# A convolution mixer and a token MLP on one core: sine phases in 16 bit, other loads first, diagonals on GpSimd, and a new order of all engines

## The chip, the core and the metric

The kernel runs on one core of one Trainium2 chip. The core has five engines that run side by side, each through its own queue of instructions in order: TensorE (PE in the profile; PEld is its weight load), VectorE (DVE), ScalarE (ACT), GpSimd (POOL) and SyncE (SP), which here only issues transfers. POOL and ACT issue transfers too. Matrix products land in PSUM, eight banks of 512 float32 per partition, and must be copied out by DVE or ACT before the bank is free; everything else lies in one tensor in SBUF that the program calls `arena` (so nearly all tiles in the profile have this one name; PSUM is `ps`). The metric is the device time of one execution in microseconds (us), the median of several runs.

## The reference

Part A mixes along the sequence (2048 positions, 448 channels): a layer norm of q, a shift convolution with four taps of k, a product with v, a long convolution of that with a state kernel (done by real FFTs of length 4096), a skip term, and the gate by q. Part B is an MLP over the 2048 positions (2048 to 1792 to 2048) with a layer norm ahead and a gelu between.

```
def _A_ref(q, k, v, shift_k, ssm_k, ssm_D):
    k_shift = sum over t of k_pad[:, t:t + S, :] * shift_k[:, ks - 1 - t]
    kv = k_shift * v
    kv_f = rfft2(kv_pad)                  # length 2 * S along the sequence
    kf_f = rfft2(kf_pad)                  # of the state kernel
    y = irfft2(kv_f * kf_f)[:S]
    y = y + kv * ssm_D
    return q * y
...
h = x + _A_ref(_layernorm(x), A_k, A_v, A_shift_k, A_ssm_k, A_ssm_D)
h2 = h + _B_ref(_layernorm(h), B_w1, B_b1, B_w2, B_b2)
```

## The kernel before

The FFTs are matrix products in two stages of small transforms. The sequence lies as 128 partitions by 16 rows (`R` = 16), so a tile row is 128 positions by 448 channels. The stages, by the names that the step tables use:

- `tables` computes the transform tables on the chip. `E` (f16, 32 tiles of 128 columns) is the sine of a phase (an odd frequency times the position, modulo 8192; for the cosine 2048 more): DVE makes the phases as int32, ACT takes the sine (L837 to L847). `FW` is the table of the forward second stage, `MA`, `MB`, `MN` those of the inverse (L854 to L874, on POOL, DVE and ACT). `ID` is the identity for the transposes (L810), made from an iota (L789).
- `kT` transposes the state kernel by PE (L1037), `kv` transposes k (L965) into `KX`, convolves it with the four taps as products with diagonal matrices `DG` (L991; `DG` is made at L950 from the taps `wsc`, L943), and multiplies by v (L1006, DVE).
- `k1`, `u1`: first forward stage of the state kernel and of the signal (L1058; copied out by L1066 and L1068, then exchanged between partitions by 48 transfers each way, L1074, two of three on POOL and one on SP). Four buffers in SBUF take the copies, so the fifth group waits for transfers.
- `k2`, `u2`: second forward stage (L1093, needs `FW`; copied out by L738, L739, L741, L742).
- `i1`: the product of the two spectra (L1160, DVE, 16 of 1.08 us) and the first inverse stage (L1177), then an exchange by L1201 and, for the last rows, L1188.
- `i2`: second inverse stage (L1303, L1309), gate and residual, layer norm statistics and the normalised row `Q` (L1388). `q` are the statistics of the first layer norm (L1237 to L1260).
- `mlp`: first product (L1435 for 7 of 14 column blocks, row by row as `Q` comes; L1445 for the others), gelu (L1425), second product (L1457, 16 output rows of 14 products), the end of each row (L1460) and its store (L1468, L1471, L1465).

No planner decides at build time. Each instruction belongs to a step (`tables.6`, `kv.4`) and has a number in it; the table `ORDER` lists, for each engine, every instruction in the order of that engine's queue, and the table `SLOTS` says which PSUM bank each use takes. `_Sched` replays the tables, works out which semaphores each instruction must wait for, and emits the engines' programs. Which of DVE and ACT copies a PSUM bank out (`FX`) is set by the table in which the copy stands. An instruction that waits holds all that stands behind it on its engine.

Loads are issued by SP in the order of its table: two of the four pieces of k, the four of the state kernel, the row `ssm_D`, the two biases, the other k, v and the taps. `b2` is cast to float32 on DVE (L938). The first-layer weights (L1408, L1412) and the second-layer weights (L1419) follow late.

## Time and profile before

| what | us |
|---|---|
| median of 3 runs (170.71 to 171.06) | 170.73 |
| span of the profiled execution, first to last instruction | 168.7 |
| busy PE, DVE, ACT, POOL in that span | 160.0, 101.7, 90.3, 58.8 |
| PE starts the first product of the MLP | 78.26 |
| PE starts the second product | 123.70 |

The span lies inside the time of a run; what lies around it is 170.73 - 168.7 = 2.0 us. The profile has an entry for each instruction, named by its line, with its start, its duration and what ended the idle time of its engine before it. "Busy" of PE counts the pipeline's latency with each product, so PE may be called busy while it waits a little between short products. The granted TensorE clock is full (9 in each of 40 slices).

### The profile page before, as it was taken

Reading aid. Unit: us, or ns where it says so; the run is one execution under the profiler, and the core shown is the slowest. Engines: PE = TensorE matmul, PEld = TensorE weight load, DVE = VectorE, ACT = ScalarE, POOL = GpSimd, SP = SyncE. Lnnn points to the kernel's source line nnn. Section 1 sums busy time; section 2 is a strip of 40 time slices with the busy share of each in tenths; the row PEclk is TensorE's granted clock in tenths of the full one; section 3 lists DMA queues with packets and bytes.
Section 4 is the critical chain, followed back from the end, with each engine's and each line's share of the span. In section 5 each row is a group of like instructions: output and inputs, shape, how many; then the busy total and the mean of one; then the engine's idle time right before and its main releaser. Section 6 shows DMA issues by size and latency. Waiting matters only on the chain.

```text
span 168.7 us, 3563 instructions
## 1 busy us (share of the span) xinstructions
PE 160.0 (95%) x1416; PEld 92.4 (55%) x1416; DVE 101.7 (60%) x191; ACT 90.3 (54%) x130; POOL 58.8 (35%) x155
## 2 busy tenths in 40 slices
PE   6999999979989989889999999999999999999994
PEld 2776745434333333344554545555577777777783
DVE  7998999989999999999987440000002313132231
ACT  3699847989999999999675803103640000000000
POOL 8345727685830555675777330000000000000000
PEclk9999999999999999999999999999999999999999
DMA  4999899893659766658999999920000111101111
GB/s 142 421 310 385 286 278 348 312 355 132 211 134 325 248 197 186 196 152 290 388 402 400 424 421 422 418 112 0 0 0 12 46 54 54 54 2 56 54 54 54
DMA packets 15564, 35.15 MB, mean 208 GB/s; under 512 B 3804, under 2 KB 9644, under 8 KB 15548
## 3 DMA queue, kind: packets, MB, share of 16 engines
q1 hardware_dynamic: 12396, 28.26, 46.1%
q0 software_dynamic: 3008, 6.58, 12.1%
q8 instruction: 11, 0.18, 0.4%
q10 hardware_dynamic: 144, 0.08, 0.2%
q14 instruction: 5, 0.04, 0.1%
HBM read 22.05 MB, written 1.84 MB: 142 GB/s over the span
## 4 chain that ended last, share of the span: by engine, by line
PE 62%; ACT 15%; DVE 10%; DMA 6%; issue 3%; POOL 1%; DVEq 0%; ACTq 0%; POOLq 0%
PE ps L1457 25%; PE ps L1435 13%; PE ps L1445 13%; ACT arena L738 7%; DMA arena<-arena 6%; ACT arena L1068 4%; ACT arena L739 4%; DVE arena L1160 2%; PE ps L1309 2%; PE ps L1058 2%; PE ps L1037 2%; PE ps L1093 2%; DVE arena L741 2%; DVE arena L837 1%; PE ps L1177 1%
## 5 line engine op out<-in xcount | busy, mean ns | idle before, releaser
L1460 DVE SCALAR_TENSOR_TENSOR arena<-ps,arena 128x448 bf16<-128x448 f32 (+2 forms) x17 | 11.1, 656 | 55.8 <-PE ps L1457 55.8
L1457 PE MATMUL ps<-arena 128*128 128x448 bf16 (+2 forms) x238 | 42.7, 342 | 0.0
L1457 PEld LDWEIGHTS ps<-arena 128*128 128x128 bf16 x238 | 33.3, 145 | 9.5
L1435 PE MATMUL ps<-arena 128*128 128x448 bf16 x112 | 23.5, 353 | 0.0
L738 ACT CAST arena<-ps 128x896 bf16<-128x896 f32 (+1 forms) x29 | 23.1, 933 | 0.0
L1068 ACT CAST arena<-ps 128x896 bf16<-128x896 f32 x24 | 20.2, 920 | 4.8 <-PE ps L1058 3.3
L1445 PE MATMUL ps<-arena 128*128 128x448 bf16 x112 | 22.3, 352 | 0.0
L1074 POOL DMA_DIRECT2D arena<-arena x32 | 17.7, 558 | 8.6 <-ACT arena L1068 8.5
L1425 ACT ACTIVATE arena<-ps,arena 128x448 bf16<-128x448 f32 x14 | 8.2, 632 | 19.3 <-PE ps L1445 10.3
L1093 PE MATMUL ps<-arena 128*64 128x448 bf16 x128 | 15.3, 361 | 2.0 <-ACT arena L739 0.9
L1435 PEld LDWEIGHTS ps<-arena 128*128 128x128 bf16 x112 | 10.7, 98 | 10.8 <-DVE arena L1388 1.3
L1445 PEld LDWEIGHTS ps<-arena 128*128 128x128 bf16 x112 | 11.0, 98 | 10.2
L1160 DVE TENSOR_TENSOR arena<-arena 128x1792 bf16<-128x1792 bf16 x16 | 16.5, 1084 | 0.0
L1177 PE MATMUL ps<-arena 64*128 64x448 bf16 x128 | 14.1, 351 | 1.1 <-ACT arena L738 0.5
L1058 PE MATMUL ps<-arena 128*32 128x448 bf16 x256 | 14.6, 355 | 0.5 <-ACT arena L1068 0.2
L1201 POOL DMA_DIRECT2D arena<-arena x16 | 9.3, 586 | 13.8 <-ACT arena L738 12.9
L1093 PEld LDWEIGHTS ps<-arena 128*64 128x64 f16 x128 | 5.3, 108 | 11.2 <-ACT arena L739 3.4
L1177 PEld LDWEIGHTS ps<-arena 64*128 64x128 f16 x128 | 5.2, 94 | 9.8 <-DVE arena L1160 3.1
L1388 DVE TENSOR_SCALAR arena<-arena 128x448 bf16<-128x448 f32 x16 | 7.6, 509 | 4.8 <-POOL arena L1381 4.8
L1058 PEld LDWEIGHTS ps<-arena 128*32 128x32 f16 x256 | 5.1, 95 | 7.8 <-ACT arena L1068 2.6
L1237 DVE BATCH_NORM_STATS2 arena<-arena 128x6 f32<-128x448 bf16 x16 | 9.4, 612 | 0.0
L739 ACT ACTIVATE arena<-ps 128x896 bf16<-128x896 f32 x10 | 8.6, 926 | 0.8 <-PE ps L1093 0.8
(99 smaller groups left out, 189.4 us busy)
## 6 DMA issues: line engine op xcount, KB each, us to landing
arena<-in_B_w_dram SPq DMA_DIRECT2D x8, 896.0 KB, 10.2
arena<-in_B_w_dram SPq DMA_DIRECT2D x2, 2048.0 KB, 17.3
arena<-arena SPq DMA_DIRECT2D x16, 224.0 KB, 3.7
arena<-arena POOLq DMA_DIRECT2D x32, 112.0 KB, 3.9
arena<-in_B_w_dram SPq DMA_DIRECT2D x2, 1536.0 KB, 19.1
arena<-arena POOLq DMA_DIRECT2D x13, 196.0 KB, 3.7
arena<-in_A_k_dram SPq DMA_DIRECT2D x4, 448.0 KB, 5.9
arena<-in_A_v_dram SPq DMA_DIRECT2D x4, 448.0 KB, 9.1
```

The lines of the kernel that those rows point to most:

```text
L738: return e.copy(out=dst(), in_=src())
L739: return e.activation(out=dst(), in_=src(), func=ACT.Copy, scale=scale)
L1058: op("pe", lambda e, W, b=b, r=r, q=q, x=x, c0=c0: e.matmul(PS[32 * q:32 * q + 32, b.slots[x], 0:D], E[:, 2 * r + x, c0:c0 + 32], src[:, r ...
L1068: return e.copy(out=dst, in_=Ppair(b)) if W == "act" else e.tensor_copy(out=dst, in_=Ppair(b))
L1074: shuf[tag].append(op(q_, lambda e, W, g=g, i=i, a=a, nu=nu, jh=jh: e.dma_start(T[a + i:a + i + 4 * nu - 3:4].rearrange("p (j k) c d -> p ...
L1093: op("pe", lambda e, W, b=bs[h], h=h, j=j, c=c, par=par: e.matmul(PS[64 * par:64 * par + 64, b.slots[c], 0:D], FW[:, 64 * c:64 * c + 64], ...
L1160: op("dve", lambda e, W, m=m, i=i: e.tensor_tensor(out=MR(m.slots[0]).rearrange("p (x y) d -> p x y d", x=2), in0=TU[:, i].unsqueeze(2).br ...
L1177: k = op("pe", lambda e, W, b=bs[h], m=ms[h], par=par, t=t, tab=tab, xy=xy, P=P: e.matmul(Pb(b, par), tab[P, :], MR(m.slots[0])[P, xy, :], ...
L1435: op("pe", lambda e, W, r=r, fc=fc, b=bs[fc]: e.matmul(Pb(b), W1A[:, r, 128 * fc:128 * fc + 128], Q[:, r, :], start=(r == 0), stop=(r == R ...
L1445: op("pe", lambda e, W, r=r, fc=fc, b=b: e.matmul(Pb(b), W1B[:, r, 128 * (fc - n0):128 * (fc - n0) + 128], Q[:, r, :], start=(r == 0), sto ...
L1457: op("pe", lambda e, W, r=r, fc=fc, b=b, d0=d0, d1=d1: e.matmul(Pb(b)[:, d0:d1], W2[fc // 7][:, fc % 7, r:S:R], G[:, fc, d0:d1], start=(fc ...
L1460: op("dve", lambda e, W, r=r, b=b, A=A, d0=d0, d1=d1: e.scalar_tensor_tensor(out=XR(r)[:, d0:d1], in0=Pb(b)[:, d0:d1], scalar=bm[:, r:r + ...
```

## The change

Four things change in the code, and with them every row of `ORDER` and `SLOTS`.

- The phases of `E` are int16. A row of frequencies (`frow`) is multiplied once by the position within its residue (`bq`), masked and shifted to make row 0 (`ph[:, 0]`), and rows 1 to 15 follow by doubling: rows m to 2m-1 are rows 0 to m-1 plus m times the frequency row (`f2`, `f4`, `f8`). The cosine's phase is its own tile (`a0`), so three operations of 1024 elements per half stand for the add and the mask, and each half's sine is two instructions of 1024 in place of one of 2048.
- The state kernel is loaded first. The taps are loaded by ACT's queue in rows, transposed by four small PE products and copied out; the biases are loaded later. `b2` is used as it is, without the cast.
- `DG` may stand on DVE or POOL, and stands on POOL.
- `ORDER` and `SLOTS` are new throughout. In the MLP the products of several rows now alternate between banks.

```diff
-            for h in range(2):
...
-                op("dve", lambda e, W, h=h, ph=ph: e.tensor_tensor(
-                    out=ph[:, 1], in0=frow.unsqueeze(1).broadcast_to([128, 8, 128]),
-                    in1=srow[:, 8 * h:8 * h + 8].unsqueeze(2).broadcast_to([128, 8, 128]), op=ALU.mult),
...
+            op("dve", lambda e, W: e.tensor_tensor(out=bq, in0=frow, in1=qcol.broadcast_to([128, 128]), op=ALU.mult),
...
+            op("dve", lambda e, W: e.tensor_scalar(out=ph[:, 0], in0=bq, scalar1=511, scalar2=4, op0=ALU.bitwise_and,
+                                                   op1=ALU.logical_shift_left),
...
+            for m, (fm, o_) in ((1, (frow, o_fr)), (2, (f2, o_f2)), (4, (f4, o_f4)), (8, (f8, o_f8))):
+                op("dve", lambda e, W, m=m, fm=fm: e.tensor_tensor(
+                    out=ph[:, m:2 * m], in0=ph[:, 0:m], in1=fm.unsqueeze(1).broadcast_to([128, m, 128]), op=ALU.add),
...
+                    out=a1[:, 8 * h:8 * h + 8], in0=ph[:, 8 * h:8 * h + 8], scalar1=8191, scalar2=None, op0=ALU.bitwise_and),
...
+                    out=a0[:, 8 * h:8 * h + 8], in0=ph[:, 8 * h:8 * h + 8], scalar1=2048, scalar2=None, op0=ALU.add),
...
+                    out=a0[:, 8 * h:8 * h + 8], in0=a0[:, 8 * h:8 * h + 8], scalar1=8191, scalar2=None, op0=ALU.bitwise_and),
...
+                for c, (src, o_src_) in enumerate(((a0, o_a0), (a1, o_a1))):
+                    op("act", lambda e, W, h=h, c=c, src=src: e.activation(
...
-            for i, c in enumerate((0, 1, 2, 3)):
+            for i, c in enumerate((3, 0, 1, 2)):
...
-            op(Dq, lambda e, W: e.dma_start(wsn[:, 0:3], A_shift_k[0:384].rearrange("(c p) j -> p c j", p=128)),
+            op("act", lambda e, W: e.dma_start(wsn[0:3], A_shift_k[0:384].rearrange("(c p) j -> c (p j)", c=3)),
...
-            op("dve", lambda e, W: e.tensor_copy(out=b2c, in_=b2n), r=[(o_b2n, 32)], w=[(o_b2c, 64)], n=16)
...
-            op("pool", lambda e, W: e.tensor_copy(out=wsc, in_=wsn.rearrange("p c j -> p (c j)")),
+                op("pe", lambda e, W, b=b, j=j: e.transpose(out=Pbf(b, 0)[:, 4 * j:4 * j + 4], in_=wsn[0:4, j:512:4],
...
-            op("dve", lambda e, W: e.tensor_tensor(
+            op(("dve", "pool"), lambda e, W: e.tensor_tensor(
                 out=DG.rearrange("p c j d -> p (c j) d"), in0=I2.unsqueeze(1).broadcast_to([128, 16, 64]),
...
-        "dummy.0:1-9 kv.4:0-11 kv.3:0-7 kv.6:0-11 kv.5:0-7 kT.1:0-7 kT.0:0-3 kT.1:9-11 kT.0:4-7 kT.3:0-7 "
+        "dummy.0:1-9 kT.0:0-7 kT.1:0-7 kT.1:9 kT.5:0-7 kT.4:0-7 kT.6:0-7 kT.7:0-7 kT.1:10-11 kT.2:0-7 kT.3:0-7 "
```

DVE, the start of the program. Before, the phases as int32, with small operations of the other tables between, up to the first copy of a transposed block out of PSUM:

```order
L837 TENSOR_TENSOR arena<-arena 128x1024
L822 TENSOR_TENSOR arena<-arena 128x8
L837 TENSOR_TENSOR arena<-arena 128x1024
L825 TENSOR_TENSOR arena<-arena 128x8
L841 TENSOR_SCALAR arena<-arena 128x1024
L828 TENSOR_TENSOR arena<-arena 128x1
L841 TENSOR_SCALAR arena<-arena 128x1024
L828 TENSOR_TENSOR arena<-arena 128x1
L844 TENSOR_SCALAR arena<-arena 128x2048
L831 CAST arena<-arena 128x6
L844 TENSOR_SCALAR arena<-arena 128x2048
L741 COPY arena<-ps 128x8x128
```

DVE at the same place now; L875 are the doublings, L882, L885 and L888 the masks and adds, L842 is `ID`, L999 half of `DG`'s making, L768 the first copy of a transposed block:

```order
L872 TENSOR_SCALAR arena<-arena 128x128
L875 TENSOR_TENSOR arena<-arena 128x256
L875 TENSOR_TENSOR arena<-arena 128x512
L885 TENSOR_SCALAR arena<-arena 128x1024
L882 TENSOR_SCALAR arena<-arena 128x1024
L842 TENSOR_SCALAR arena<-arena 128x128
L999 TENSOR_TENSOR arena<-arena 128x64
L888 TENSOR_SCALAR arena<-arena 128x1024
L875 TENSOR_TENSOR arena<-arena 128x1024
L885 TENSOR_SCALAR arena<-arena 128x1024
L888 TENSOR_SCALAR arena<-arena 128x1024
L768 COPY arena<-ps 128x8x128
```

The identity, made first before, now stands behind the first half's phases, and the small operations of the other tables have gone to some thirty rows further on.

POOL, before the exchanges of the first stage (L1074). Before, all tables are done there:

```order
L854 TENSOR_SCALAR arena<-arena 128x128 x3
L858 TENSOR_TENSOR arena<-arena 128x384
L871 TENSOR_TENSOR arena<-arena 128x128 x3
L874 TENSOR_SCALAR arena<-arena 128x128
L943 CAST arena<-arena 128x16
L1074 DMA arena<-arena 8x4x1792 x26
L1245 TENSOR_SCALAR arena<-arena 128x2
```

POOL at the same place now; L1001 makes `DG`, L1125 are the exchanges, the IOTA and MEMSET rows belong to the other tables:

```order
L838 IOTA arena 128x16
L821 IOTA arena 128x128
L1001 TENSOR_TENSOR arena<-arena 128x1024
L853 MEMSET arena 128x1 x2
L852 MEMSET arena 128x1
L1125 DMA arena<-arena 8x4x1792
L816 MEMSET arena 128x1
L1279 MEMSET arena 128x1
L852 MEMSET arena 128x1 x2
L825 IOTA arena 128x128
L1125 DMA arena<-arena 8x4x1792
```

The exchanges now stand behind `DG`, which waits for the taps, and the table operations (the former L854, L858, L871, L874) stand among the exchanges. The taps' copy (`kv.0:4`) stands on DVE behind the copies of `k1.0` and `k1.1`, one of `kv.5`, two aggregates and a statistic.

SP, around the first weights (L1408 before, L1459 now) and the exchanges of `i1` (L1201 and L1188 before, L1252 and L1239 now). Before:

```order
L1126 DMA arena<-arena 8x256 x4
L1201 DMA arena<-arena 8x2x896 x11
L1201 DMA arena<-arena 8x14x896
L1188 DMA arena<-arena 8x14x448 x2
L1408 DMA arena<-in_B_w_dram 128x4x896 x3
L1412 DMA arena<-in_B_w_dram 128x4x896 x4
```

Now:

```order
L1177 DMA arena<-arena 8x256 x4
L1239 DMA arena<-arena 8x14x448 x2
L1252 DMA arena<-arena 8x2x896
L1459 DMA arena<-in_B_w_dram 128x4x896
L1252 DMA arena<-arena 8x2x896
L1459 DMA arena<-in_B_w_dram 128x4x896 x2
L1252 DMA arena<-arena 8x2x896 x9
L1459 DMA arena<-in_B_w_dram 128x4x896
L1463 DMA arena<-in_B_w_dram 128x4x896 x4
```

Nine of the eleven small exchanges, which carry rows 14 and 15 of the last inverse stage, now stand behind two loads of weights that wait for the exchanges of L1239. On PE, row 14 of that stage (`i2.93`) stands behind 43 products counted from the first of the MLP. At the end of PE's queue the last narrow products (`mlp.39:26-29`, 128 columns) are 4 instead of 7 (`mlp.39:23-29`) behind the last wide one (`mlp.39:13`), and the last full row ends right ahead of them (`mlp.35:13`, then five wide products).

More of the change, by code (lines that the diff above doesn't have):

```diff
@@ L751, in emit_tables @@
             NB = 3 * 128
-            o_fr = small(512)
-            o_s = small(64)
+            o_fr = small(256)
+            o_f2, o_f4, o_f8, o_bq = [o_TK + 8192 + 256 * k for k in range(4)]
+            o_s = small(16)
             o_p = small(80)
-            frow = view(o_fr, [128], i32)
-            srow = view(o_s, [16], i32)
+            frow, f2, f4, f8 = [view(o, [128], i16) for o in (o_fr, o_f2, o_f4, o_f8)]
+            qcol = view(o_s, [1], i16)
+            bq = view(o_bq, [128], i16)
             pc = view(o_p, [12], i32)
@@ L923, in _build @@
         o_b2n = small(32)
-        o_b2c = small(64)
         o_b1c = small(64)
@@ L927, in _build @@
         b2n = view(o_b2n, [16])
-        b2c = view(o_b2c, [16], f32)
         b1c = view(o_b1c, [16], f32)
```

85 lines of the change are left out of this document (52 added, 33 removed), and 194 rows, old and new, of tables (ORDER, SLOTS).

## Prediction

> **What bounds the kernel.** First the page's busy times, then the engines in three stretches, cut where DVE begins the phases, where it first copies from PSUM, and where it writes the first normalised row:
>
> ```profile
> span 168.7 us, 3563 instructions
> PE 160.0 (95%) x1416; PEld 92.4 (55%) x1416; DVE 101.7 (60%) x191; ACT 90.3 (54%) x130; POOL 58.8 (35%) x155
> ...
> 2.23:8.35 6.12, 6.12 (x62) 3.79 (x61) 6.12 (x12) 2.82 (x4) 3.45 (x20) 1.00 0.96 375
> 8.35:77.68 69.33, 64.49 (x877) 31.87 (x875) 66.34 (x112) 63.56 (x78) 39.06 (x74) 1.00 0.77 251
> 77.68:168.70 91.02, 88.50 (x479) 56.28 (x477) 28.22 (x68) 22.68 (x50) 14.66 (x38) 1.00 0.43 169
> ```
>
> The columns are the stretch, its length, and the busy time of PE, PEld, DVE, ACT and POOL. From 77.68 on PE is the limit. Before, DVE is: 66.34 of 69.33, idle for 2.99, with ACT close behind at 63.56, idle for 5.77. Both empty PSUM banks, so the early stages go at their pace, and PE's 64.49 is partly latency of short products. The chain of work that ended last says the same:
>
> ```profile
> 2.25 1.21 DVE arena L837
> ...
> 21.55 6.04 DMA arena<-arena
> ...
> 48.09 4.21 ACT arena L738 x6
> ...
> 77.76 0.43 DVE arena L1388
> ...
> 78.26 1.10 PE ps L1435 x5
> ...
> 123.70 42.08 PE ps L1457 x231
> 165.78 0.03 issue
> 165.81 0.55 DVE arena L1460
> ```
>
> It begins with the phases on DVE, passes an exchange and many copies, and from 78.26 lies on PE. The second product is 224 products of 448 columns in 42.08, 0.188 each; PE has no room there, whatever the order of the products. So the change is worth what it moves the start of the MLP, plus the tail.
>
> **Term 1, the phases and DG on DVE.** These rows give the prices (last columns: busy in us and mean in ns, then idle before):
>
> ```profile
> L837 DVE TENSOR_TENSOR arena<-arena 128x1024 int32<-128x1024 int32 x2 | 2.4, 1223 | 0.0
> L841 DVE TENSOR_SCALAR arena<-arena 128x1024 int32<-128x1024 int32 x2 | 1.4, 686 | 0.0
> L844 DVE TENSOR_SCALAR arena<-arena 128x2048 int32<-128x2048 int32 x2 | 2.4, 1224 | 0.0
> L950 DVE TENSOR_TENSOR arena<-arena 128x1024 bf16<-128x1024 bf16 x1 | 1.2, 1217 | 0.0
> L938 DVE CAST arena<-arena 128x16 f32<-128x16 bf16 x1 | 0.2, 165 | 0.0
> L860 DVE TENSOR_SCALAR arena<-arena 128x384 int32<-128x384 int32 x1 | 0.4, 365 | 0.1
> L866 DVE TENSOR_SCALAR arena<-arena 128x128 f32<-128x128 int32 x2 | 0.6, 282 | 0.0
> L1160 DVE TENSOR_TENSOR arena<-arena 128x1792 bf16<-128x1792 bf16 x16 | 16.5, 1084 | 0.0
> ```
>
> Removed: the six phase operations are 2 x 1.22 + 2 x 0.69 + 2 x 1.22 = 6.3; by the clock they fill the stretch of 6.12 less some 0.37 for the small ones between, 5.75. DG (L950) 1.22 and the cast L938 0.17 go too: 7.14 in all. Added: 16-bit work. For an operation on two tensors, L1160 (16 bit) costs 1084/1792 = 0.60 ns an element and L837 (32 bit) 1.19, half. So the four doublings of 128, 256, 512 and 1024 elements, at 0.16 fixed and 0.52 ns an element, are 0.23 + 0.29 + 0.42 + 0.69, and the product `bq`, whose one factor is a single column, 0.29 at the 32-bit rate: 1.92. For an operation with constants no row is 16 bit. L860 and L841 give (686 - 365)/640 = 0.50 ns an element and 0.17 fixed in 32 bit; halved as for two tensors, 1024 elements are 0.43. The ends are 0.28 (L866, 128 elements) and 0.69 (L841, no gain). I take 0.43, since the halving is what the nearest pair shows: six are 2.6 (1.7 to 4.1), three of 128 elements 0.6. Sum 5.1; with all at the high ends, the doublings at the 32-bit rate too, 7.7. The phases start about 0.25 later, as three frequency rows and a column must come from POOL first. Term: -7.14 + 5.1 + 0.25 = -1.8 (-2.7 to +0.8).
>
> **Term 2, what the order moves onto DVE ahead of the first row of the MLP.** Counting both programs' DVE queues up to that row (L1388 before):
>
> ```profile
> L741 DVE CAST arena<-ps 128x896 bf16<-128x896 f32 x4 | 4.3, 1085 | 0.4 <-PE ps L1093 0.2 <-PE ps L1177 0.2
> L741 DVE COPY arena<-ps 128x1024 bf16<-128x1024 bf16 x11 | 7.2, 684 | 0.3 <-PE ps L1037 0.3
> L1237 DVE BATCH_NORM_STATS2 arena<-arena 128x6 f32<-128x448 bf16 x16 | 9.4, 612 | 0.0
> L1239 DVE BATCH_NORM_AGGREGATE arena<-arena 128x2 f32<-128x6 f32 x16 | 2.1, 164 | 0.0
> L1339 DVE SCALAR_TENSOR_TENSOR arena<-ps,arena 128x448 f32<-128x448 f32 x4 | 2.6, 678 | 0.4 <-PE ps L1309 0.4
> ```
>
> Two more copies of 896 float32 (+2.17), two fewer of 1024 bf16 (-1.37), one more statistic (+0.61) and two aggregates (+0.33), one L1339 fewer (-0.68), the taps' copy (+0.17, as L938): +1.2. With term 1, DVE has 0.6 less to do.
>
> **Term 3, idle time.** The waits of DVE and ACT in 8.35 to 77.7:
>
> ```profile
> DVE arena L741 <- PE ps L1037: 0.6, 2, 0.3
> ...
> ACT arena L1068 <- PE ps L1058: 3.3, 5, 2.3
> ```
>
> The first are waits for transposes of the state kernel; loaded first, it should be there while DVE still makes phases, so I take 0.5 off; the ends are none and 2.0 of the 2.99. ACT has more to do: two copies of 896 go and two of 1024 come, about even, but the sine is four pieces, and three transfers are issued there:
>
> ```profile
> L847 ACT ACTIVATE arena<-arena 128x2048 f16<-128x2048 int32 x2 | 3.9, 1999 | 0.0
> L862 ACT ACTIVATE arena<-arena 128x384 f32<-128x384 int32 x1 | 0.6, 617 | 0.0
> ...
> 6.87 0.45 SPq L890 DMA_DIRECT2D arena<-in_A_shift_k_dram  x1
> ```
>
> A line through L862 and L847 gives 1.15 for 1024, so 4.6 against 4.0; with 3 x 0.45 (SP's issue; none is on ACT early) that is +2.0. I price it at nothing, because ACT's 5.77 of idle time covers it and its sine may start some 3 us earlier than 8.47; without that cover it costs up to 2.0. The second half's sine and the copy of `kT.3` are queued behind these issues; `k1.8`, which needs both, is the fourth group of `k1`, so they have time. The four small transposes and the earlier q loads on SP, ahead of k, I also price at nothing, since PE and the transfers are behind DVE there; the k pieces that `kv.4` needs come sixth in the queue.
>
> **Term 4, the tail.** Three narrow products of 128/448 x 0.188 = 0.05 no longer cover the copy of the last wide piece, and the last full row's store is issued just ahead of the last: +0.2 (0 to +0.6). Inside the MLP: nothing, with the loads of term 5 in time.
>
> **Sum.** -1.8 + 1.2 - 0.5 + 0.2 = -0.9 on the profiled span, 167.8; the run median lies 2.0 above the span, so 170.73 - 0.9 = 169.8.
>
> **Term 5, two queues that hide now.** POOL first:
>
> ```profile
> 16.34 1.36 POOL L1074 DMA_DIRECT2D arena<-arena  x2 [0.36 <-ACT arena L1068]
> ...
> 16.30:46.20 29.90, 28.05 (x524) 14.54 (x520) 28.52 (x44) 24.69 (x30) 19.70 (x37) 1.00 0.80 278
> ...
> L858 POOL TENSOR_TENSOR arena<-arena 128x384 int32<-128x384 int32 x1 | 1.0, 1002 | 0.1
> L871 POOL TENSOR_TENSOR arena<-arena 128x128 f16<-128x128 f32 x3 | 1.3, 455 | 3.5 <-ACT arena L862 3.5
> ...
> 7.42 1.33 POOL L854 TENSOR_SCALAR arena<-arena 128x128 int32<-128x128 int32 x1 [2.67 <-DVE arena L831]
> 8.75 0.72 POOL L854 TENSOR_SCALAR arena<-arena 128x128 int32<-128x128 int32 x2
> ...
> 7.21 1.23 DVE L844 TENSOR_SCALAR arena<-arena 128x2048 int32<-128x2048 int32 x1
> ```
>
> DG on POOL by the line of L871 and L858 (2.1 ns an element) is 2.4 (ends 1.2, as on DVE, and 8.6, below). It waits for the taps' copy on DVE, by the DVE order about 16 us in, so the first exchange leaves at some 18 instead of 16.34. From 16.3 to 46.2, all exchanges of the first stages, POOL is idle for 10.2. Into that go DG 2.4 and the tables: L854 1.1, L858 1.0, L871 1.4, and about 1.7 of small ones, 7.6 in all. So 2.6 of its idle time is left; I price it at nothing on that, and it is thin.
>
> The page "GPSIMD Engine Reference" of the Trainium skill, section 1 (Specifications), says that GpSimd shares its SBUF interfaces with VectorE and contends with VectorE instructions that use both ports or two SBUF inputs. The trace bears this out: L854's first took 1.33 while L844 ran, the next two 0.72 together once L844 had ended. By that rule DG would take 2.4 x 1.33/0.36 = 8.6 if DVE did only such work beside it, and the sum would be as late as the second rival below; DVE's neighbours there are copies from PSUM, which the rule spares, so the sum stays.
>
> SP second:
>
> ```profile
> 75.20 1.47 SPq L1408 DMA_DIRECT2D arena<-in_B_w_dram  x3
> ...
> L1201 SPq DMA_DIRECT2D arena<-arena x12: 666/666/683, 54.6 to 69.2; - x12
> ...
> DMA to landing us min/median/max: 3.1/3.7/4.2
> ```
>
> The exchanges of rows 14 and 15 follow two weight loads: 2 x 0.49 + 9 x 0.67 = 7.0, and 3.7 to land, 10.7 after the wait that ended at 75.20. PE needs row 14 at 78.26 - 75.20 + 43 x 0.188 = 11.1. Just in time.
>
> **Rivals.** (a) The new order also takes the idle time: DVE's 2.99 falls to 1.0, 1.5 more than in the sum, 168.3 (168 to 169). For it speaks ACT's 5.77 of idle time; against it, that every bank must still be emptied by these two. (b) Slower: POOL becomes the limit of the exchanges. It decides once POOL still waits more than 2.6 in all between 16 and 46; if half of its 10.2 of waits stay, it ends 2.5 late and so does the MLP, 172.3. For it: in-order waits for the taps and for table steps on DVE; against: that earlier `k1` groups feed it better. (c) 16 bit brings nothing: 169.8 + 2.6 = 172.4. Against it stands L1160. (d) Rows 14 and 15 late, or the tail at its end: +0.5 to +1.5, 170.3 to 171.3. (e) It cancels: 170.7.
>
> **Chances and range.** The sum 0.42 (169.0 to 170.3), (a) 0.18, (b) 0.19, (c) 0.07, (d) 0.10, (e) 0.04. About 0.2% is what a measurement of this kernel can tell from no change. Faster: sum and (a), 0.60. Same: (e) and 0.03 of (d), 0.07. Slower: the rest, 0.33. The range takes in most of (a) and the middle of (b): 168.0 to 172.3, leaving out some 0.2.
>
> **What would show it.** The six 1024-element operations at 0.43 rather than 0.69; first copy of a transposed block from DVE at about 7 us; DVE's idle time from there to the first normalised row under 2.5; DG at 2.4 and POOL's first exchange near 18; the first MLP product at 77.0 to 77.4; no wait of PE for a transfer at row 14. The prediction is wrong if the first product of the MLP comes after 78.3, most likely through exchanges that leave POOL late, or if PE waits within the MLP.

## The result

The changed kernel takes 180.34 us (median of 4 runs, 178.38 to 181.13) where the kernel before, on the same chip, takes 170.89 (170.71 to 171.35): a ratio of 1.0492, 95% interval 1.0407 to 1.0577. It is slower by about 9.5 us; the ratio and its interval leave out the run of 181.13, which counts as slow, and the median of the other three is 179.67, 8.8 above before. The granted clock of TensorE, averaged over the span, was 1.00 in the run of 178.38, 0.99 in that of 179.67 and 0.98 in the two above 181: how much the dip described below costs differs from one execution to the next, and with a full clock the kernel is still 7.5 above before. The profiled execution took 181.01 for a span of 179.2, so what lies around the span is 1.8, about as before (2.0); the span has grown by 10.5. The page's first lines and its rows of the granted clock and of the transfers, of after:

```profile
span 179.2 us, 3577 instructions
...
PE 163.8 (91%) x1420; PEld 93.3 (52%) x1420; DVE 100.7 (56%) x197; ACT 91.7 (51%) x133; POOL 65.5 (37%) x157
...
PEclk9999999999999999985899999999999999999999
DMA  5999679789660355799699999940000000002026
```

The work is nearly the same (DVE 100.7 for 101.7, ACT 91.7 for 90.3). What is new is time in which the engines wait, and a dip in the clock row, which was flat. Where the time lies is read from the engines by stage; the cuts are PE's first product of the first inverse stage `i1`, its last, the first product of `i2` that needs an exchange, the first of the MLP, and 20 us behind that. After:

```profile
core 0: us, PE busy (x) PEld busy (x) DVE busy (x) ACT busy (x) POOL busy (x), PEclk, DMA share, GB/s
...
54.00:71.30 17.30, 15.24 (x151) 6.82 (x152) 17.30 (x23) 15.70 (x20) 10.48 (x14) 1.00 0.36 105
71.30:78.60 7.30, 3.97 (x38) 2.23 (x34) 3.41 (x11) 6.10 (x8) 6.01 (x10) 1.00 0.82 212
78.60:86.40 7.80, 7.06 (x21) 2.83 (x22) 6.44 (x21) 2.79 (x6) 1.91 (x4) 0.56 0.98 345
86.40:106.40 20.00, 18.63 (x95) 8.29 (x93) 12.51 (x35) 14.10 (x34) 14.00 (x35) 1.00 0.96 363
```

The same stages before:

```profile
51.40:69.60 18.20, 17.11 (x154) 6.23 (x156) 17.99 (x24) 18.20 (x23) 7.76 (x14) 1.00 0.74 243
69.60:73.40 3.80, 3.29 (x32) 1.71 (x27) 3.80 (x12) 3.75 (x6) 3.78 (x8) 1.00 0.65 187
73.40:78.20 4.80, 4.31 (x27) 2.17 (x27) 4.43 (x15) 4.67 (x8) 2.31 (x4) 1.00 0.51 149
78.20:98.20 20.00, 19.98 (x106) 9.97 (x106) 15.08 (x45) 13.93 (x34) 13.90 (x38) 1.00 1.05 405
```

| stretch | before | after | more |
|---|---|---|---|
| start to first product of `i1` | 51.4 | 54.0 | +2.6 |
| `i1` | 18.2 | 17.3 | -0.9 |
| `i1`'s end to the first product of `i2` that needs its exchange | 3.8 | 7.3 | +3.5 |
| from there to the MLP's first product | 4.8 | 7.8 | +3.0 |
| MLP, first to last product | 87.7 | 89.9 | +2.1 |
| behind the last product | 2.7 | 2.9 | +0.2 |

Three things stand in these rows. During `i1` the transfers run at a share of 0.36 instead of 0.74, and at 0.82 behind it, when PE and DVE wait for them (busy for 3.97 and 3.41 of 7.30): the exchanges have been pushed together to the end. The stretch after that has a granted clock of 0.56. And in the first 20 us of the MLP, PE does 95 products where it did 106; 11 at 0.19 are 2.1, the MLP's whole loss. PE at this place, by its timeline, after and before:

```profile
69.97 1.69 PE L1228 MATMUL ps<-arena 64*128 64x448 bf16 x16 [1.89 <-POOL arena L1190]
...
78.64 0.94 PE L1360 MATMUL ps<-arena 128*128 128x448 bf16 x4 [3.17 <-DMA arena<-arena]
80.28 5.41 PE L1360 MATMUL ps<-arena 128*128 128x448 bf16 x14 [0.70 <-DMA arena<-arena]
...
86.44 1.11 PE L1486 MATMUL ps<-arena 128*128 128x448 bf16 x5
```

```profile
75.23 2.82 PE L1309 MATMUL ps<-arena 128*128 128x448 bf16 x14 [0.49 <-DMA arena<-arena]
```

After a wait of 3.17 for an exchange the same 14 products take 5.41 instead of 2.82: 2.6 of the 3.0 of that stretch is the clock. The chain of work that ended last goes through it, where before it was on PE, DVE and PE again:

```profile
73.48 6.75 DMA arena<-arena
80.28 5.41 PE ps L1360 x14
...
99.00 1.12 POOL arena L1432
106.01 1.37 DVE arena L1439 x3
```

The waits of after, by who is waited for (total, times, longest):

```profile
POOL arena L1001 <- DVE arena L768: 13.1, 1, 13.1
DVE arena L1439 <- POOL arena L1432: 7.5, 6, 2.3
...
PE ps L1360 <- DMA arena<-arena: 3.9, 2, 3.2
...
PE ps L1228 <- POOL arena L1190: 1.9, 1, 1.9
```

L1001 is `DG`, L1439 writes a normalised row `Q`, L1432 is the power (of minus one half) that gives its scale, L1360 is `i2`, L1228 `i1`. The rows for the phases came out as priced, by their groups on DVE:

```profile
L872 DVE TENSOR_SCALAR arena<-arena 128x128 int16<-128x128 int16 x2 | 1.7, 1510 | 0.0
L875 DVE TENSOR_TENSOR arena<-arena 128x128 int16<-128x128 int16 x1 | 1.5, 1505 | 0.0
L885 DVE TENSOR_SCALAR arena<-arena 128x1024 int16<-128x1024 int16 x2 | 0.9, 426 | 0.1
...
L875 DVE TENSOR_TENSOR arena<-arena 128x1024 int16<-128x1024 int16 x1 | 0.7, 685 | 0.0
```

1024 elements with constants take 0.43 and the last doubling 0.69. Only the three smallest operations, which run at 2.3 to 4.0 us beside POOL's own first operations, were held (1.5 each, overlapping, about 1.4 together). Why is not shown: in `e11` below the same three, at 2.65 to 3.3 and also beside POOL's first operations, took 0.19, 0.22 and 0.35. The first copy of a transposed block starts at 7.65 rather than 8.35.

### The profile page after: what moved, and what is told of

Same layout as the page of the kernel before. It is cut to its first block, busy times and chain, and to the rows that moved or that the text cites. A ratio compares the mean times of both kernels' runs of the same rounds, so it can differ in the third digit from the quotient of the medians.

```text
span 179.2 us, 3577 instructions
## 1 busy us (share of the span) xinstructions
PE 163.8 (91%) x1420; PEld 93.3 (52%) x1420; DVE 100.7 (56%) x197; ACT 91.7 (51%) x133; POOL 65.5 (37%) x157
## 4 chain that ended last, share of the span: by engine, by line
PE 54%; POOL 13%; ACT 10%; DMA 10%; issue 5%; DVE 5%; SPq 1%; POOLq 0%; DVEq 0%; ACTq 0%
PE ps L1508 23%; PE ps L1496 11%; DMA arena<-arena 10%; ACT arena L765 7%; PE ps L1486 4%; PE ps L1109 4%; PE ps L1360 3%; PE ps L1016 2%; PE ps L1088 2%; POOL arena L1432 2%; POOL arena L1252 2%; POOL arena L1125 2%; PE ps L1042 2%; ACT arena L1119 2%; DVE arena L1439 1%
## 5 line engine op out<-in xcount | busy, mean ns | idle before, releaser
L1508 PE MATMUL ps<-arena 128*128 128x448 bf16 (+2 forms) x238 | 45.4, 343 | 0.0
L1511 DVE SCALAR_TENSOR_TENSOR arena<-ps,arena 128x448 bf16<-128x448 f32 (+2 forms) x17 | 10.5, 652 | 58.8 <-PE ps L1508 58.8
L1508 PEld LDWEIGHTS ps<-arena 128*128 128x128 bf16 x238 | 33.0, 145 | 10.7 <-DVE arena L1511 0.5
L1486 PE MATMUL ps<-arena 128*128 128x448 bf16 x112 | 25.8, 353 | 1.3 <-DVE arena L1439 1.1
L1496 PE MATMUL ps<-arena 128*128 128x448 bf16 x112 | 26.4, 353 | 0.0
L765 ACT CAST arena<-ps 128x896 bf16<-128x896 f32 (+1 forms) x28 | 22.3, 921 | 2.1 <-PE ps L1228 1.6
L1125 POOL DMA_DIRECT2D arena<-arena x32 | 18.1, 569 | 3.6 <-ACT arena L1119 2.7
L1486 PEld LDWEIGHTS ps<-arena 128*128 128x128 bf16 x112 | 10.3, 98 | 13.3 <-DVE arena L1439 4.6
L1211 DVE TENSOR_TENSOR arena<-arena 128x1792 bf16<-128x1792 bf16 x16 | 16.7, 1088 | 0.3 <-DMA arena<-arena 0.3
L1144 PE MATMUL ps<-arena 128*64 128x448 bf16 x128 | 14.7, 358 | 2.2 <-DMA arena<-arena 1.1
L1496 PEld LDWEIGHTS ps<-arena 128*128 128x128 bf16 x112 | 10.9, 98 | 9.6 <-ACT arena L1476 0.4
L1109 PE MATMUL ps<-arena 128*32 128x448 bf16 x256 | 15.6, 356 | 0.1
L1228 PE MATMUL ps<-arena 64*128 64x448 bf16 x128 | 13.5, 351 | 2.3 <-POOL arena L1190 1.9
L1360 PE MATMUL ps<-arena 128*128 128x448 bf16 x32 | 10.4, 460 | 4.0 <-DMA arena<-arena 3.9
L1252 POOL DMA_DIRECT2D arena<-arena x16 | 9.5, 599 | 10.0 <-ACT arena L765 9.8
L1439 DVE TENSOR_SCALAR arena<-arena 128x448 bf16<-128x448 f32 x16 | 7.7, 512 | 7.5 <-POOL arena L1432 7.5
L1144 PEld LDWEIGHTS ps<-arena 128*64 128x64 f16 x128 | 6.0, 109 | 10.7 <-ACT arena L766 2.8
L1370 ACT ACTIVATE arena<-ps,arena 128x448 f32<-128x448 f32 x10 | 7.1, 721 | 7.8 <-PE ps L1360 7.4
L1228 PEld LDWEIGHTS ps<-arena 64*128 64x128 f16 x128 | 5.6, 94 | 9.6 <-DVE arena L1211 3.5
L765 ACT COPY arena<-ps 128x1024 bf16<-128x1024 bf16 (+1 forms) x9 | 9.0, 1017 | 2.1 <-PE ps L1016 1.8
## 6 DMA issues: line engine op xcount, KB each, us to landing
arena<-in_B_w_dram SPq DMA_DIRECT2D x2, 2048.0 KB, 17.3
```

The costliest lines, as they stand in the source:

```text
L765: return e.copy(out=dst(), in_=src())
L1109: op("pe", lambda e, W, b=b, r=r, q=q, x=x, c0=c0: e.matmul(PS[32 * q:32 * q + 32, b.slots[x], 0:D], E[:, 2 * r + x, c0:c0 + 32], src[:, r ...
L1125: shuf[tag].append(op(q_, lambda e, W, g=g, i=i, a=a, nu=nu, jh=jh: e.dma_start(T[a + i:a + i + 4 * nu - 3:4].rearrange("p (j k) c d -> p ...
L1144: op("pe", lambda e, W, b=bs[h], h=h, j=j, c=c, par=par: e.matmul(PS[64 * par:64 * par + 64, b.slots[c], 0:D], FW[:, 64 * c:64 * c + 64], ...
L1211: op("dve", lambda e, W, m=m, i=i: e.tensor_tensor(out=MR(m.slots[0]).rearrange("p (x y) d -> p x y d", x=2), in0=TU[:, i].unsqueeze(2).br ...
L1228: k = op("pe", lambda e, W, b=bs[h], m=ms[h], par=par, t=t, tab=tab, xy=xy, P=P: e.matmul(Pb(b, par), tab[P, :], MR(m.slots[0])[P, xy, :], ...
```

## The experiments

In the diffs a step and its instruction numbers stand as in `ORDER`; a kernel is called here by the first part of its label. A new PE order also meant new PSUM banks, except in `e2`, `e3`, `e4` and `e8`, which keep those of after, and `e11`, `e14` and `e16`, with those of before. The theories are: the new order is the cause (and then which part of it), or the code is (16 bit, taps by PE, `DG` on POOL).

**Order or code.** The changed code in the order of before:

```diff
-    ORDER, SLOTS of after
+    ORDER of before: phases, four loads and four small transposes fitted in, taps' loads first on ACT, DG on DVE
```

> The changed code (phases in 16 bit, taps turned on TensorE, loads of the taps on ACT) in the order of before on all engines, with DG on DVE. Theory A, the loss lies in the new order (what POOL's queue holds back, and TensorE's half clock behind it): 169.5 to 171.5, first MLP product at 77.5 to 78.8, clock 1.0. Rival B, the new code itself is slow (16-bit work next to POOL, four pieces of sine, transfers on ACT): 174 or more, first MLP product after 81.

172.41 against 170.81, ratio 1.0098 (1.0059 to 1.0137). It lies between the two forecasts, much nearer to "order": some 8 of the 9.5 us are the order, and 1.6 are the code with its loads. `i2` starts at 75.3, the MLP at 80.1 and lasts 87.7, all at full clock.

**Causes in the order that I suspected first.** POOL's queue around the last exchanges of `i1`:

```diff
-pool: ... i1.4:21 q.4:4 ... i1.8:21 ew.0:1 ... q.4:5 i1.4:19 i1.6:20
+pool: ... ew.0:3 ew.0:1 ... i1.6:19 i1.4:19 i1.6:20 ... i1.16:22 q.4:4
```

> The changed kernel with six POOL instructions moved at the end of i1: the copy of a table that i1.16 needs goes up to its two sister copies, the statistics step that was held for 2.54 us goes behind the last exchange, two exchanges go up. Theory A: the last i1 products no longer wait 1.9 for the copy, i2 begins some 2 to 4 earlier (75 to 77), TensorE's wait ahead of i2 falls under 2 and its clock stays at 1.0; time 174 to 177. Rival C, the late start has its cause in the transfers' own landing (some 6 us, however early they are issued) or in DVE and ACT: 178 to 181, i2 not before 78.

180.64, ratio 1.0609 (1.0544 to 1.0674). The wait of 1.9 for L1190 is gone (0.3 for DVE's product, L1211, is left there), and another one took its place:

```profile
PE ps L1354 <- DMA arena<-arena: 4.5, 2, 2.4
```

L1354 waits for the fills of the last table (L1177 on SP). The limit moved; nothing was gained, and the clock was halved at 74 to 80 us instead.

`DG` on DVE, and the taps' loads first on ACT's queue:

```diff
-pool: tables.1:0 kv.1:3
+dve:  kv.0:4 kv.1:3
```

> The changed kernel with DG back on DVE, right behind the taps' copy. Theory A: POOL's 13.1 of waiting goes, its first exchange leaves by 16.5 instead of 19.17, k2 begins 1 to 2 earlier than 37.34 and the time is 177 to 179. Rival C, DVE sets the pace there and pays 1.2 for it: k2 begins no earlier, 180 to 182.

```diff
-act: ... kT.1:8 loads.4:2 ... tables.8:3 loads.4:1 ... tables.8:4 loads.4:0
+act: loads.4:0-2 ...
```

> The changed kernel with ACT's three transfers of the taps ahead of the sines (they stand behind three of the four sines now). Theory A: the taps' copy on DVE, and with it DG on POOL, comes 3 to 5 earlier than 17.2, POOL's first exchange leaves at about 15, k2 begins about 2 earlier and the time falls by 2 to 178. Rival C: the copy still stands behind k1.1 on DVE, DG starts no more than 1 earlier, and the time stays at 180.

180.59, 1.0558 (1.0506 to 1.0609), and 180.65, 1.0570 (1.0525 to 1.0616). Without `DG`, POOL's first exchange leaves at 14.8 instead of 19.2, yet the second stage of the state kernel starts no earlier (38.2, after 37.3; `e8`, with the front of after, has 38.9, so that this start varies by 1.6 between executions). So the 13.1 that POOL waits for the taps, the largest wait ahead of the MLP, is not by itself what delays the front. The second was a miss: `DG` still came at 18.7, because its copy on DVE stands behind other work.

**The queue of fills and the order of SP.** The last table's transposes and fills early; then SP's exchanges ahead of the weight loads too; then POOL's moves on top:

```diff
-pe: i1.12:8 ct0.0:0-7           sp: ct0.1:0 i1.4:18
+pe: u1.15:7 ct0.0:0-7           sp: ct0.1:5 i1.4:18
```

> The changed kernel with the eight transposes for rows 0 and 1 (ct0) put ahead of k2.14 instead of behind i1.12, their copy ahead of k2.15's, and the four transfers that need them (EW, 67.45 now) right behind the two that clear the place. The rest of SP's queue is left. Theory D, SP's queue: its exchanges and the first weights wait behind late things, the transfer engines stand at 0.42 from 49.5 to 69.6 and at 0.87 to 1 behind that, so the last exchanges land 6 late instead of 3.7. SP is then still held by the copy of i1.4 (62) and of i1.16 (72), so D expects little: 178.5 to 180. Theory A, POOL's queue alone: no change, 180 to 181.

```diff
+sp: ct0.1:5 w1a.0:0 i1.1:20 i1.1:22 i1.4:18 i1.10:20 i1.10:22 i1.14:20 i1.14:22 i1.8:20 i1.8:22 i1.12:20 i1.12:22 i1.6:22
```

> e5_fill_early with SP's exchanges of i1 in the order in which their rows become ready, the first weight block ahead of them and i1.16's behind them. Theory D: the transfer engines are busy over 0.6 from 49.5 to 69.6, the last exchanges land in about 4, i2 begins at 75 to 76.5, TensorE's clock stays at 1.0, the first MLP product comes at 80.5 to 83 and the time is 174.5 to 177. Theory A: i2's start stays with POOL's bunched exchanges, at 78 or later, and the time at 179.5 to 181.

> e6_sp_order and the six POOL moves of e2_pool_i1 together. Theory D with A as its second half: i2 begins at 73.5 to 75, first MLP product at 79 to 81.5, time 172.5 to 175. If POOL's order is without effect here too: as e6_sp_order within 0.5. If neither queue is the cause: 179 or more.

182.12 (1.0607, 1.0531 to 1.0683), 182.20 (1.0653, 1.0618 to 1.0688) and 180.46 (1.0548, 1.0471 to 1.0625). None gains. With SP in order the small exchanges do leave during `i1`, and PE still waits 3.5 for one; with both queues repaired the exchanges of 196 KB take 6.2 to land (median) in place of 4.0. So it is not one entry in one queue that is late. I read it as the last groups of `i1` coming out of PSUM together, which the order of `i1` below tests.

**The clock.** Sixteen more idle-filling products (their result is read by nothing) where PE waits for the exchange:

```diff
-pe: ct.2:7 ... i2.41:1 warm.1:0
+pe: ct.2:7 warm.1:0 warm.2:0 ... warm.17:0
```

> The changed kernel with 16 more products of one table and a block of zeros, whose result nobody reads, behind the last transposes ahead of i2, where TensorE waits 3.17 for a transfer. Theory K, the wait itself halves the granted clock: it stays at 1.0 from 78 to 87, the fourteen products of i2 take 2.8 instead of 5.41, the first MLP product comes at about 84 and the time is 177.5 to 178.5, and the spread of the runs shrinks. Rival: the clock falls for another reason, and nothing changes, 179.5 to 181.

179.36, ratio 1.0481 (1.0427 to 1.0536). Its stretch of the first two `i2` groups, then its PE:

```profile
78.60:86.40 7.80, 7.30 (x38) 3.24 (x36) 6.18 (x21) 4.94 (x11) 2.60 (x6) 1.00 0.96 311
```

```profile
79.61 4.42 PE L1362 MATMUL ps<-arena 128*128 128x448 bf16 x20
```

The clock stays full, 20 products take 4.42, and the MLP starts at 84.4 instead of 86.4. That the low clock follows PE's wait is thereby shown. Little of it is seen in the time: this kernel is 8.1 above its own before, after 9.5, less than the 2 to 3 expected, and the intervals of the two ratios overlap. In its profile k2 started 1.6 later (38.9 for 37.3), and the MLP's first 20 us hold 91 products where after has 95.

**The order of `i1`.** DVE makes the products of the spectra in the order `i1.0`, `i1.1` (both for PE's `i1.1`), `i1.9`, `i1.10` and so on; PE's table began with `i1.10:1-8`, which needs the third of them, and took the halves of a pair apart. Here PE, ACT and POOL take them in DVE's order:

```diff
-pe: u2.13:3 i1.10:1-8 i1.1:1-8 i1.1:10-17 i1.4:0-7 u2.5:0-3 u2.4:0-3 i1.10:10-17 i1.14:1-8 i1.4:9-16 i1.14:10-17
+pe: u2.13:3 i1.1:1-8 i1.1:10-17 i1.10:1-8 i1.10:10-17 i1.4:0-7 i1.4:9-16 u2.5:0-3 u2.4:0-3 i1.14:1-8 i1.14:10-17
```

> The changed kernel with the products of i1 in the order in which DVE makes their inputs: the two halves of each pair side by side on TensorE (i1.1, i1.10, i1.4, then two groups of u2, then i1.14; the first now stands behind the first half of i1.10 and waits for DVE's third product), ACT's copies in the same order, POOL's exchanges too. Theory E, the pairs become whole late and in a bunch, so 14 exchanges of 196 KB go out from 58.3 to 72.7 instead of 54.9 to 69.5 and the last land 6 late: POOL's first exchange at 55 to 56, i2 begins 1.5 to 3 earlier than 78.6, 176.5 to 179. Rival A or D alone (one queue's late entries): no change, 179.5 to 181.

177.35 against 170.65, ratio 1.0402 (1.0333 to 1.0471): the largest gain of the kernels that keep after's order in the main. POOL's first exchange did not come earlier (58.7; expected 55 to 56), and `i1` ends at the same time (71.4), but the exchanges at its end leave in smaller batches. POOL around `i1`'s end, after:

```profile
64.39 2.54 POOL L1296 TENSOR_SCALAR arena<-arena 128x4 f32<-128x4 f32 x1
66.87 1.83 POOL L1252 DMA_DIRECT2D arena<-arena  x3
68.69 1.14 POOL L1190 COPY arena<-arena 128x288 f16<-128x288 f16 x1
69.79 2.92 POOL L1252 DMA_DIRECT2D arena<-arena  x5
```

and POOL and PE in this kernel:

```profile
67.02 0.59 POOL L1252 DMA_DIRECT2D arena<-arena  x1 [0.52 <-ACT arena L765]
67.61 0.88 POOL L1190 COPY arena<-arena 128x288 f16<-128x288 f16 x1
68.65 1.76 POOL L1252 DMA_DIRECT2D arena<-arena  x3 [0.16 <-issue]
```

```profile
79.02 2.82 PE L1360 MATMUL ps<-arena 128*128 128x448 bf16 x14 [1.17 <-DMA arena<-arena]
```

Three in a row instead of five, PE waits 1.5 (for a late fill, L1354) and 1.2 (for an exchange) in place of 3.2 and 0.7, the clock stays full, and the 14 products take 2.82 again. The MLP starts at 82.3 instead of 86.4; 2.6 of these 4.1 are the clock. That the smaller batches are the reason is read from these rows and not shown: `e10` below has the same order of `i1` and waits as long as after.

On this base, SP's and POOL's moves, the early fills, and the MLP's order of before (its products, copies and stores):

```diff
+e10: the pe, sp and pool moves of e7          e12: the pe and sp moves of e5
+e13: every mlp step of pe, act, dve and sp in the order of before
```

> e9_i1_order and e7_sp_pool together: order of i1, fills and exchanges of SP early, POOL's six moves. Theory E with D and A as further parts: i2 begins at 74 to 76, TensorE waits under 1.5 ahead of it, clock 1.0, first MLP product at 79 to 81.5, 172.5 to 175.5. If the loss is elsewhere (DVE or ACT late through the whole of i1): i2 not before 77.5, 178 or more.

> e9_i1_order with the transposes, the copy and the four fills for rows 0 and 1 early, as in e5_fill_early; the rest of SP's queue left. In e9_i1_order TensorE still waits 1.5 for such a fill ahead of i2 and 1.2 behind it. If the late fill is what is left at this place: that wait goes, the first MLP product comes at 80.5 to 81.8 instead of 82.3, 175.5 to 176.7. If the landing of the exchanges stands right behind it: no change, 177 to 178.

> e9_i1_order with the MLP's products, its copies and its stores in the order of before (product groups one behind the other instead of mixed). From the first MLP product to the last, e9_i1_order takes 90.2 and the kernel before 87.7. If the mixed order costs this: 87.7 to 88.5, time 175 to 176. If the rows of Q come too late for either order: 90 and 177 to 178.

178.66 (1.0463, 1.0398 to 1.0528), 177.90 (1.0428, 1.0373 to 1.0484) and 177.65 (1.0388, 1.0335 to 1.0441). The moves bring nothing, as they did on after; in the first the exchanges of 196 KB took 5.6 to land, PE waited 3.0 again and its clock fell to 0.72 (80 to 86 us). The mixed order of the MLP's products is not the cause of its loss either: with the old one it lasts 90.7.

**The code by itself.** The kernel before with only the phases in 16 bit; then its `DG` on POOL; then its state kernel loaded first; then the taps on ACT's queue with `DG` on POOL; then in that one some of the state kernel's transposes earlier on PE:

```diff
+e11: phases in int16 as in the change, all else as before
+e14: e11 and  pool: kv.0:0 kv.0:4       (DG behind the taps' copy)
+e15: e11 and  sp: loads.0:0 loads.1:0 loads.2:0 loads.3:0 first, kT ahead of kv on pe
+e16: e11 and  act: loads.4:0-2 first, pool: kv.0:0 kv.0:4 tables.9:8
+e17: e16 and  pe: kv.4:0-11 kv.3:0-7 kT.1:0-7 kT.0:0-3 kv.6:0-11 kT.1:9-11 kT.0:4-7 kv.5:0-7
```

> The kernel before with one part of the change alone: phases in 16 bit by doubling and the sine in four pieces. Loads, taps, DG and all other orders as before. By the prediction's first term without DG and the taps' cast (7.14 less 1.39 removed, 5.1 added, 0.25 later): DVE copies its first transposed block about 0.4 earlier and the time is 170.0 to 170.8. Theory B, the 16-bit code costs time (held beside POOL, four pieces on ACT): 171.3 to 173, as e1_order_undone.

> e11_16bit_alone with the taps' cast and DG on POOL ahead of its table products, in its wait for ACT (9.2 to 14.2), so that neither DVE nor an exchange waits for it. If DVE sets the pace of the early stages: 1.2 less on DVE, 169.6 to 170.4. If TensorE and the copies of ACT take over: 170.7 to 171.3 as e11_16bit_alone. If POOL next to DVE makes both slower: over 171.5.

> e11_16bit_alone with the four pieces of the state kernel loaded first and the first of their transposes ahead of those of k. In e11_16bit_alone DVE ends the phases at 7.17 and waits 0.72 for the first transposes. If that wait is what swallows the gain of the phases: first copy at 7.2, 169.5 to 170.5. If the later pieces land late in turn, as in the runs of the changed kernel where the first k1 product came between 11.7 and 13.3: 171 to 172.5.

> e14_16bit_dg_pool with the three transfers of the taps first on ACT, which is idle until 5.7, instead of on SP behind the first v piece: in e14_16bit_dg_pool POOL waited 6.4 for them and DG ran at 15.9, in front of the exchanges. If DVE sets the pace of the early stages: DG runs at 9.5 to 12 on POOL, the first exchange leaves at 16.1 as before, DVE has 1.22 less, 169.3 to 170.3, under both kernels. If the copies of ACT and TensorE take over: 170.6 to 171.3.

> e16_taps_act_dg_pool with the transposes of the state kernel's first two groups put between those of k on TensorE, the loads as before. In e11_16bit_alone DVE waits 0.72 for them after the phases. If that wait is on the path: 0.4 to 0.7 under e16_taps_act_dg_pool. If the pieces of the state kernel have not landed by 6.5, TensorE and with it the copies of k on ACT stand: 0.3 to 1.5 over it.

| kernel | us | ratio (95%) |
|---|---|---|
| e11, 16 bit alone | 171.19 | 1.0028 (1.0001 to 1.0055) |
| e14, and `DG` on POOL | 172.97 | 1.0117 (1.0084 to 1.0149) |
| e15, and the state kernel first | 179.02 | 1.0457 (1.0412 to 1.0503) |
| e16, and taps on ACT, `DG` on POOL | 171.55 | 1.0039 (1.0018 to 1.0060) |
| e17, and transposes earlier | 172.85 | 1.0132 (1.0099 to 1.0166) |

With 16 bit alone DVE is through with the phases at 7.17 instead of 8.35, and then waits for PE's transposes of the state kernel:

```profile
6.75 0.42 DVE L852 TENSOR_SCALAR arena<-arena 128x1024 int16<-128x1024 int16 x1
7.89 0.69 DVE L738 COPY arena<-ps 128x1024 bf16<-128x1024 bf16 x1 [0.72 <-PE ps L1053]
```

Taking `DG` away as well (1.22) gives the same answer; in `e16` this wait is

```profile
DVE arena L737 <- PE ps L1052: 2.6, 2, 1.5
```

Loading the state kernel first (`e15`) lets DVE start at 7.09, and then k comes late: ACT waits for k's transposes, PE for k itself. Its clock fell too (0.78 from 8 to 12 us, 0.76 from 12 to 30), so not all of its loss is k's lateness.

```profile
ACT arena L734 <- PE ps L980: 8.9, 2, 6.9
...
PE ps L980 <- DMA arena<-in_A_k_dram: 1.8, 1, 1.8
```

In `e17` PE's weight loads (L1051) wait 1.2 for the load of the state kernel, and the time is 1.3 above `e16`: the second forecast. So in the first 20 us the loads and PE's transposes set the pace together with DVE, and work taken from DVE alone is worth nothing. `e14` shows what a late exchange can cost. In its profile, whose clock is full up to there, POOL waited 6.4 for the taps, its first exchange left at 19.5 instead of 16.1 (as in `e11`), and some 1.7 us were lost against `e11` (each by its own before) although DVE had 1.22 less to do.

**Front or back.** Last, the order of before up to the end of `i1`, and the new order from there:

```diff
 pe, act, dve, pool, sp:
-    after's rows up to i1.16's products
+    before's rows up to i1.16's products (pe: 884 of 1420), then after's rows without these
```

> The changed code with the order of before on every engine up to the end of the first inverse stage (up to i1.16's products on PE, 884 of its 1420 instructions, and what stands ahead of that point in time on the other engines; DG on DVE there), and the changed order from there on: the copies and exchanges of the last group, the second inverse stage, the normalised rows and the MLP. PSUM banks are dealt out anew. The question is which half of the order holds the 5 us that the repaired i1 leaves. If it is the front (the stages up to i1), this kernel stands near the one with the whole order undone, 172.4: 172 to 173.5, the MLP's first product at 80 to 81 and 87.7 to 88.5 from its first to its last product. If the back has its own price (rows of the MLP late whatever stands ahead), 174 to 176, with 89.5 to 90.5 from the first to the last product of the MLP.

174.69 against 170.45, ratio 1.0257 (1.0210 to 1.0304): the second forecast. The MLP starts at 79.0, earlier than with the whole order undone, and lasts 90.7 instead of 87.7. DVE at the rows `Q` (L1434 here), in this kernel and then in before (L1388):

```profile
82.46 0.94 DVE L1434 TENSOR_SCALAR arena<-arena 128x448 bf16<-128x448 f32 x2 [0.90 <-POOL arena L1427]
...
86.77 0.94 DVE L1434 TENSOR_SCALAR arena<-arena 128x448 bf16<-128x448 f32 x2 [0.87 <-POOL arena L1427]
...
90.08 0.51 DVE L1434 TENSOR_SCALAR arena<-arena 128x448 bf16<-128x448 f32 x1 [1.17 <-POOL arena L1427]
```

```profile
81.56 0.48 DVE L1388 TENSOR_SCALAR arena<-arena 128x448 bf16<-128x448 f32 x1
...
83.87 0.96 DVE L1388 TENSOR_SCALAR arena<-arena 128x448 bf16<-128x448 f32 x2
...
87.41 0.51 DVE L1388 TENSOR_SCALAR arena<-arena 128x448 bf16<-128x448 f32 x1 [0.60 <-POOL arena L1381]
```

Each row's scale is a chain of five small operations on POOL (some 3 us) between two visits of DVE. Before, DVE has the next row's gate to do in that time, and its second pair of rows with POOL's work ends at 83.9 + 0.96, 6.6 us into the MLP; here it stands and waits, and the same rows are there at 86.77 + 0.94, 8.7 into it. PE has no row: in the first 20 us of the MLP it does 90 products (95 in after, 106 before); 16 at 0.19 are the 3.0 lost. In which order POOL takes the operations of that second pair adds to it, in `e18` and then in before:

```profile
82.82 0.21 POOL L1416 TENSOR_TENSOR arena<-arena 128x2 f32<-128x2 f32 x1
83.56 1.40 POOL L1294 TENSOR_TENSOR arena<-arena 128x4 f32<-128x4 f32 x1 [0.53 <-DVE arena L1291]
84.93 0.41 POOL L1418 TENSOR_TENSOR arena<-arena 128x2 f32<-128x2 f32 x1
```

```profile
81.59 0.20 POOL L1370 TENSOR_TENSOR arena<-arena 128x2 f32<-128x2 f32 x1
81.93 0.20 POOL L1372 TENSOR_TENSOR arena<-arena 128x2 f32<-128x2 f32 x1
```

In the new order a step of another chain, `q.8:5` (L1294), stands between the second and the third operation, and POOL waits for DVE ahead of it: 1.9 pass between these two operations, against 0.14 before, which is 1.8 of the 2.1 by which the pair is late. In after the same step lies on the chain of work that ended last (1.42 at 90.41). No kernel here moved it alone, so this is read from the rows and not tested.

By the medians, each against the runs of the kernel before taken beside it, and if the parts simply add: the code 1.6; the order behind `i1` 4.2 - 1.6 = 2.6; the order of `i1`'s products, with the clock that falls after it, 9.5 - 6.7 = 2.8 (0.8 by the run of after with a full clock, 7.5 - 6.7, so that some 2 of it would be the clock); and the order ahead of `i1`, by what is left, 2.5. No kernel here beats the one before.

## Why the prediction was wrong

- **"So the change is worth what it moves the start of the MLP, plus the tail."** The measure was right, the sum wrong by sign: the MLP's first product came at 86.44, not 77.0 to 77.4. This one number holds 8.2 of the 10.5.
- **Term 1 (-1.8).** Its sizes hold: 0.43, 0.29, 0.42, 0.69. What failed is the step from busy time to end time: "Before, DVE is [the limit]: 66.34 of 69.33". `e11` and `e16` took 1.2 and 2.4 off DVE and the time did not fall (ratios 1.0028 and 1.0039). An engine that is 96% busy, with ACT at 92% and PE near it, was here one of several that take turns; the next wait took the gain.
- **Term 2 (+1.2) and term 3 (-0.5).** The counts of term 2 hold; term 3 failed. Between the phases and the first row `Q`, DVE has 0.3 us more of work than before (72.78 for 72.46) and stands idle for 8.0 us where before it was 2.99 and 2.5 was forecast: a gain of 0.5 became a loss of 5. From 75.0 to 78.6 alone it does nothing at all, behind PE's wait for the exchanges. The order was counted (which operations came ahead of the row) and not followed (in which sequence the groups of `i1` are needed). That count doesn't show that PE's first group waits for DVE's third product, nor that the exchanges bunch. The first of these was not what held `i1`: `e9` is without it, and its `i1` starts no sooner (55.2).
- **Term 4.** The tail is right: 2.9 for 2.7, the +0.2 forecast. "Inside the MLP: nothing" failed: +2.1 in after and +3.0 in `e18`. I had looked at PE's products and the loads of term 5, not at DVE's rows `Q` with POOL's chain between them, which pace PE in its first 20 us, nor at the place of POOL's step `q.8:5` within that chain.
- **Term 5, "I price it at nothing".** For POOL's first stage that was about right: the first exchange left at 19.2 (forecast 18) and `DG` took 1.91 (forecast 2.4), and removing it (`e3`) brings nothing. Of POOL's idle time from 16.3 to 46.6 there is 5.0 left, more than the 2.6 at which rival (b) was to decide and about the half for which it gave 2.5 late. POOL's last exchange of that stage ended 1.0 late (47.2 for 46.2), and PE's first product of `i1` came 2.6 late. The chain of after runs through POOL's exchanges there (35.77 to 40.51), with a step of its tables among them (L917, 0.62), but that of `e9`, with the same rows there, does not. Whether that is rival (b)'s wait stays open. For rows 14 and 15 on SP it was right: PE waits for no transfer there. The same queues failed one stage later, at `i1`'s end, a place that the prediction did not price.
- **Rival (b)** had the sign and the kind ("exchanges that leave POOL late", and "if PE waits within the MLP"), at another place, and the price was short: 172.3 for 180.3. It left out the halved clock that such a wait sets off (2.6), and a second loss in the MLP (2.1).
- The Trainium skill, page "GPSIMD Engine Reference", section 1, was weighed in the prediction against `DG`, with 8.6 by its rule (2.4 x 1.33/0.36 is 8.9). Measured: 1.91 beside DVE's copies (L768) and a product that reads PSUM (L1117), neither of which has two SBUF inputs (whether L768 uses both ports, the trace doesn't say). Where DVE does read two SBUF inputs the trace agrees with the rule: L1296, of 128 x 4, took 2.54 at 64.39 beside DVE's products L1211, and 0.24 at 73.89 when they were over.

What stays open: which move ahead of `i1` costs its 2.5 us. There k2 starts at 37.3 in after and at 35.1 in `e18`; `DG` (`e3`) and the taps' loads (`e4`) were tried and are not it, alone; POOL's steps of the tables among the exchanges were not tried alone. Nor was the place of `q.8:5` in the MLP. The kernels' other PSUM banks are mixed into these differences. The decomposition is a difference of medians with intervals of some 1 us each.

## What to carry to other kernels

Before pricing work removed from a busy engine, look at who would be waited for next; where several engines are over 90% busy, as DVE and ACT were here, assume the gain is zero until a row shows slack. When a whole order is replaced, follow the sequence in which one stage's results are consumed by the next (here DVE's products, PE's groups, the exchanges, the rows of the MLP), since a count of instructions ahead of a point says nothing on bunching. And price a wait of TensorE with what comes behind it: here 3 us of wait cost up to another 2.6 in clock.

## What the runs showed of the hardware that was not expected

- TensorE was busy 0.47 of the 3.6 us from 75.0 to 78.6; its granted clock then averaged 0.56 over the next 7.8 us, and 14 products took 5.41 instead of 2.82. With extra products in the gap it stayed at 1.00 (`e8`). The page "TensorE: Matmul & The Clock Gate" of the Trainium skill, Part 1, says that the clock falls to half after an idle window of about 3.4 us and returns after as long a busy one; the trace agrees on the fall and on the half. The half clock lasted 3.4 us in `e3`, `e4` and `e10` (81.2 to 84.5 in `e4`), which is the page's figure, but 6.9 in after (79.3 to 86.2, with PE busy for 6.20 of it) and 6.8 in `e2`.
- Exchanges of 196 KB between partitions land in 3.7 (median, before), 4.0 (after) and 6.2 us (`e7`), the longest where the exchanges of both queues were moved ahead (5.2 in `e2` and `e6`, 5.6 in `e10`); the last one on the chain of after took 6.75.
- Three DVE operations of 128 16-bit elements took 1.40 to 1.62 at 2.3 us beside POOL's first operations; in `e11`, where they also run beside POOL's first operations, the same three took 0.19 to 0.35. POOL's work alone therefore doesn't explain it; the cause stays open.
